# Block-sparse attention and its expert layers on one core: scores from 64-row tiles of TensorE, and the first product cut in two around the values

## The chip, the core and the metric

One core of a Trainium2 chip runs the whole kernel as one program. The metric is the device time of one execution in microseconds (us). TensorE's granted clock is written as a share of full speed; its two levels are 1.2 and 2.4 GHz. Five engines run programs of their own, in order: PE (TensorE), DVE (VectorE), ACT (ScalarE), POOL (GpSimd) and SP (SyncE, which here only issues DMAs).

## The reference, cut to what matters

```python
B, H, S, D = 4, 8, 768, 64             # float32; block = 32, so 24 blocks
scores = q @ k^T / sqrt(D)             # kept where mask, else -1e9
# mask: blocks at most 1 apart; the first and the last block, as rows and as columns;
# and for each query block 3 sampled key blocks
attn = softmax(scores); o = attn @ v
x = o as [B*S, H*D] = [3072, 512]
h = x @ w_in                           # 512 x 2048
g = h * erf(softplus(h))
out = g @ w_out                        # 2048 x 512
```

## The kernel before, in words

**Attention, in units.** A batch has 16 units (`units`, line 775). Ten are of kind "m": one of five tiles of 128 queries (four blocks of 32, number `j`) by one of two quads of heads. A quad is two pairs of heads (`r`), a pair is two heads (`a`), and the two heads of a pair lie on partitions 0 to 63 and 64 to 127 of the transposed queries and keys. For its own block of queries each head needs 256 key columns: 96 of the three neighbouring blocks, 96 of the three sampled blocks (copied side by side into `kg` by POOL, `gather`), and 64 of the first and the last block (`key_columns`, line 554). Four units "f" (one pair each; the first and the last block, which see all 768 keys) and two units "e" (the two remaining blocks beside the end) finish the batch.

**Scores (`scores`, line 565).** The two heads of a pair are done by one product over all 128 partitions. For this the queries of a block stand block-diagonally in `qm` (line 131): 64 columns, of which 32 belong to head 0 and are zero on the partitions of head 1, and the other way round. `qm` is zeroed once; `order_q` (line 146) copies each loaded tile `qt` into its diagonal blocks with two copies of 64 partitions. An m unit is 24 products (2 pairs x 3 column parts x 4 blocks), each 128 x 64 stationary, and blocks with even and odd `j` write the two halves of the output's partitions. All operands are float32, and a float32 product is issued as two weight loads and two matmul instructions, both of the same tile, one directly behind the other. The scores of a unit take two PSUM banks of a single buffer (`ps_s`, line 94), so the next unit's scores wait until the exponentials of this one are read out.

**Behind the scores.** `soft_max` (DVE: maximum, bias), `soft_exp` (ACT: four exponentials, one rounding copy), `soft_low` (DVE: rest of the rounding), `soft_turn` (SP: transpose by DMA). Two units later `values` (line 605) multiplies with the gathered values `vb` (96 small products of 128 x 32 stationary, float16) into `po`, a single PSUM buffer, `norm` (DVE) divides, and `turn` makes the rows of the expert layers.

**Expert layers, in groups.** There are 96 groups (4 batches x 3 chunks of 256 rows x 8 parts of 256 hidden columns). `ff_first` (line 686) makes `h` (two sets `j` of 12 products with 256 columns), `ff_logs` is five ACT instructions, `ff_power` one of DVE, `ff_exp` one of ACT, `ff_gate` three of DVE, and `ff_second` (line 735), two groups later, 12 products of 512 columns.

**The order of the work** is written by hand, and every engine keeps it (`InOrder`, line 49). After the first four units and the decoding of the weights (lines 875 to 973) the loop at line 978 runs one step per group, and most steps also have a unit. On PE such a step is: first product, values, scores, second product. On DVE it is: gate of the step before, norm, maximum and bias, `order_q` of the next tile in every second unit (`next_queries`, line 804), power, rest of the output, `soft_low`. On SP it is: writes, gathers of values, query load, transposes. `until` (line 977) sets in which steps a unit starts.

Of the kernel before, what the change touches and what calls it, by code (L numbers as in the profile page):

```python
# [42 lines left out]
def sparse_attention_moe(ctx: ExitStack, tc: tile.TileContext, qT, kT, v, sampled, w_in, w_out, out):  # L43
# [86 lines left out]
    qts = {}  # L130
    qm = cp.tile([P, HP, 4, 2, BLOCK], F32, tag="qm", name="qm")
    pool.memset(qm, 0.0)

    def load_q(b, t):
        place, tag, bufs = (mo, "g", FF_LAG + 1) if b == 0 and t in (1, 2) else (ld, "qt", 1)
        qt = place.tile([P, HP, P], F32, tag=tag, name=f"qt_{b}_{t}", bufs=bufs)
        rows = qT[b].rearrange("(r t) d s -> (t d) r s", t=2)
        if t < MT:
            c = (1 + 4 * t) * BLOCK
            sp.dma_start(qt, rows[:, :, c : c + P])  # L140
        else:
# [423 lines left out]
    def scores(unit):  # L565
        kind, b, n = unit[0], unit[1], unit[2:]
        tag = "_".join(str(x) for x in unit)
        s = ps_s.tile([P, 1024], F32, tag="s", name=f"s_{tag}")
        if kind == "m":

            t, quad = n
            s4 = s.rearrange("p (h r w) -> p h r w", h=2, r=2)
            for r in range(2):
                pr = 2 * quad + r
                for part in range(3):
                    for j in range(4):
                        o = slice((j % 2) * 64, (j % 2) * 64 + 64)
                        q_ = qm[:, pr, j].rearrange("p a c -> p (a c)")
                        c, e, keys = key_columns(b, 1 + 4 * t + j, slice(0, P), pr)[part]
                        pe.matmul(s4[o, j // 2, r, c:e], q_, keys, start=True, stop=True)  # L580
            softs[unit] = (s, 4, 256)
        elif kind == "e":
            (quad,) = n
            s3 = s.rearrange("p (r w) -> p r w", r=HP)
            for r in range(2):
                for part in range(3):
                    for j in range(2):
                        o = slice(j * 64, j * 64 + 64)
                        q_ = qm[:, 2 * quad + r, j].rearrange("p a c -> p (a c)")
                        c, e, keys = key_columns(b, NB - 3 + j, slice(0, P), 2 * quad + r)[part]  # L590
                        pe.matmul(s3[o, r, c:e], q_, keys, start=True, stop=True)
# [13 lines left out]
    def values(b, t, quad):  # L605
        po = ps_po.tile([P, 4, D + 1], F32, tag="po", name=f"po_{b}_{t}_{quad}")
        for hl in range(4):
# [5 lines left out]
            for x, ln in ((0, 0), (0, 1), (1, 0)):  # L613
                for half in range(2):
                    for j in range(4):
                        if t < MT:
                            pT = pts["m", b, t, quad][:, ((j // 2) * 2 + r) * 4 + x * 2 + half]
                            col = (j % 2) * 64 + a * 32
                            vg = vb[:, slot_of[b, 1 + 4 * t + j]]
                        elif j in (1, 2):  # L620
                            pT, col = pts["e", b, quad][:, r * 4 + x * 2 + half], (j - 1) * 64 + a * 32
                            vg = vb[:, slot_of[b, NB - 4 + j]]
                        else:
                            continue
                        w = slice(c, c + D + 1) if ln == 0 else slice(c + D + 2, c + VW)
                        todo[j].append((pT[:, col : col + 32], vg[:, half, w]))
                if t == MT:
                    for k in range(KT):
                        for j in (0, 3):
                            pT, col = pts["f", b, pr][:, x * KT + k], (0 if j else 64) + a * 32  # L630
                            w = slice(c, c + D + 1) if ln == 0 else slice(c + D + 2, c + VW)
                            todo[j].append((pT[:, col : col + 32], vb[:, slot_of[b, -1 - k // 2], k % 2, w]))
# [52 lines left out]

    def ff_first(b, ch, fg):
        tag = f"{b}_{ch}_{fg}"
        isg = first_scale(b)
        h = ps_h.tile([P, W], F32, tag="h", name=f"h_{tag}")
        xT = xTs[b, ch].rearrange("p n u c -> p n (u c)")  # L690
        for j in range(FG):
            f = fg * FG + j
            hj = h[:, j * CW : (j + 1) * CW]
            for kt in range(NK):
# [5 lines left out]
                pe.matmul(hj, lo, xa, start=False, stop=kt == NK - 1)  # L700
        ffs[b, ch, fg] = (h, isg)

    ffs = {}
# [100 lines left out]
    def next_queries(m):  # L804

        b, n = divmod(m, per)
        if n < 10 and n % 2 == 1:
            order_q(b, n // 2 + 1)
            if n < 9:
                load_q(b, n // 2 + 2)  # L810
        if n == per - 1 and b + 1 < B:
            order_q(b + 1, 0)
            load_q(b + 1, 1)

    def behind(m):

        b, n = divmod(m, per)
        if b + 1 < B:
            c = b + 1
            if n == 10:  # L820
                load_q(c, 0)
            k = n if b else 2 * (n - 10) if n > 9 else -1
# [60 lines left out]
    load_q(0, 1)  # L883
    load_q(0, 2)
    for n in range(3):
# [7 lines left out]
    place_v(0, 1, 1)  # L893
    order_q(0, 0)
    have_k.add(0)
# [21 lines left out]
    scores(units[1])  # L917
    used_keys(units[1])
    gathers(0)
    for i in range(10, 16):  # L920
# [4 lines left out]
    soft_exp(units[1])  # L925
    order_q(0, 1)
    work("Qi1 Di2 Qi2 Di3 Qi3")
# [11 lines left out]
    scores(units[3])  # L939
    used_keys(units[3])  # L940
    work("Qi6 Di7 Qi7 Do0")
    set_apart()
# [13 lines left out]
    turn(*seen(units[1]))  # L956
    order_q(0, 2)
    soft_low(units[3])
# [10 lines left out]
    gathers(0)  # L969
    load_q(0, 3)  # L970
    begun = FIRST
# [6 lines left out]
    for m in range(len(groups) + FF_LAG):  # L978
# [35 lines left out]
        if unit:  # L1014
            soft_max(unit)
            next_queries(begun - 1)
        if group:
# [56 lines left out]
```

## Time and profile before

| | us |
|---|---|
| median of 3 runs (lowest, highest) | 838.58 (835.89, 844.72) |
| the profiled execution | 838.56 |
| its span in the profile | 836.8 |
| PE busy in it | 710.8 |
| ACT busy | 601.1 |
| DVE busy | 554.4 |

The profiled execution lies at the median of the runs, and 1.8 us of it lie outside the span. The first 90 us set up (loads, decoding of the weights, the first four units), the rest is the loop over the groups. The first two dozen steps of the loop still carry work on the weights.

### The profile page before, as it was taken

To read this page: it belongs to the slowest core of one execution; us is meant where nothing else is said; L and a number is where in the kernel's file an instruction comes from. 1 tells how busy PE (TensorE), PEld (TensorE's weight loads), DVE (VectorE), ACT (ScalarE), POOL (GpSimd) and SP (SyncE) were. 2 spreads that over 40 slices of the span, in tenths; PEclk is the share of its full clock that TensorE was granted. 3 is DMA by queue.
4 is the path that set the end of the run, shared out by engine and by line. 5 is a ranking of instruction groups with operands and counts; after the bars stand their busy time and mean duration, and the time that the engine had idled before them with its cause. 6 is when DMAs were issued, how large, how long until landed. Compare 5 with 4: busy or idle time off the path is not lost.

```text
span 836.8 us, 26712 instructions
## 1 busy us (share of the span) xinstructions
PE 710.8 (85%) x11100; PEld 504.8 (60%) x11100; DVE 554.4 (66%) x977; ACT 601.1 (72%) x999; POOL 123.7 (15%) x344
## 2 busy tenths in 40 slices
PE   1253637899897899899999899999999899999997
PEld 1252424566665667566777666667777576766664
DVE  3994796887764766766566676756677567654454
ACT  4654657987865766887768778868678678776774
POOL 5430111001222220100201231000111100000000
PEclk9775867989998999999999999999999999999999
DMA  8999953687899697661497886633576758211000
GB/s 325 297 257 318 243 120 90 164 207 164 172 212 209 178 205 198 186 131 45 136 216 178 210 198 192 167 79 83 117 167 166 190 103 188 53 33 40 1 27 26
DMA packets 199930, 131.61 MB, mean 157 GB/s; under 512 B 144000, under 2 KB 167168, under 8 KB 199808
## 3 DMA queue, kind: packets, MB, share of 16 engines
q1 hardware_dynamic: 196384, 118.10, 58.1%
q0 software_dynamic: 3424, 11.80, 4.3%
q8 instruction: 87, 1.43, 0.7%
q14 instruction: 35, 0.29, 0.1%
HBM read 83.88 MB, written 12.95 MB: 116 GB/s over the span
## 4 chain that ended last, share of the span: by engine, by line
PE 47%; DVE 15%; issue 12%; ACT 10%; DMA 10%; SPq 2%; POOL 2%; POOLq 1%; ACTq 0%
PE h L59 18%; PE o L59 18%; PE s_m L59 5%; DMA vb<-vtab 4%; PE po L59 3%; DVE g L59 2%; ACT pf_m L59 2%; DVE q L59 2%; DVE mx_m L59 2%; DMA vtab<-vn 2%; SPq L59 2%; ACT x L59 2%; DVE p_m L59 2%; POOL kg L59 2%; ACT q L59 2%
## 5 line engine op out<-in xcount | busy, mean ns | idle before, releaser
L59 PE MATMUL h<-xT,wi 128*128 128x256 f16 x2304 | 274.2, 276 | 14.9 <-ACT wi L59 7.5
L59 PE MATMUL o<-wo,g 128*128 128x512 f16 x1152 | 270.3, 385 | 7.9 <-DVE wo L59 4.0
L59 PEld LDWEIGHTS <-wi 128*128 128x128 f16 x2304 | 227.4, 99 | 65.5 <-ACT wi L59 8.8
L59 PEld LDWEIGHTS <-g 128*128 128x128 f16 x1152 | 110.3, 99 | 133.0 <-issue 14.8
L59 ACT ACTIVATE x<-x 128x512 f32<-128x512 f32 x288 | 181.5, 630 | 9.1
L59 POOL COPY kg<-kx 128x128 f32 x264 | 90.5, 394 | 286.2 <-PE s_m L59 183.6
L59 ACT ACTIVATE pf_m<-s_m,nb_m 128x256 f32<-128x256 f32 x160 | 62.7, 475 | 65.4 <-DVE nb_m L59 59.5
L59 DVE SCALAR_TENSOR_TENSOR q<-x,q 128x512 f32<-128x512 f32 x96 | 66.7, 695 | 61.4 <-ACT x L59 60.1
L59 ACT ACTIVATE x<-h,isg 128x512 f32<-128x512 f32 x96 | 65.2, 680 | 36.3 <-PE h L59 35.7
L59 PE MATMUL s_m<-kx,qm 128*64 128x64 f32 (+1 forms) x1280 | 75.0, 249 | 6.8 <-ACT pf_m L59 4.2
L59 ACT ACTIVATE q<-q 128x512 f32<-128x512 f32 x96 | 59.5, 620 | 29.6 <-DVE q L59 29.6
L59 DVE SCALAR_TENSOR_TENSOR q<-q,h 128x512 f32<-128x512 f32 x96 | 65.5, 682 | 22.6 <-ACT q L59 22.6
L59 DVE TENSOR_TENSOR p_m<-pf_m,p_m 128x1024 f16<-128x1024 f32 x40 | 49.3, 1232 | 32.3 <-ACT p_m L59 32.3
L59 DVE SCALAR_TENSOR_TENSOR g<-q,g 128x512 f16<-128x512 f32 x96 | 67.0, 698 | 3.3
L59 PE MATMUL po<-vb,pT_m 128*32 128x65 f16 (+1 forms) x3840 | 44.7, 201 | 25.7 <-DMA vb<-vtab 15.0
L59 PEld LDWEIGHTS s_m<-kx,qm 128*64 128x64 f32 x1280 | 59.7, 146 | 10.4 <-ACT pf_m L59 4.9
L59 ACT ACTIVATE q<-x 128x512 f32<-128x512 f32 x96 | 60.5, 630 | 3.1
L59 DVE TENSOR_REDUCE mx_m<-s_m 128x4 f32<-128x1024 f32 x40 | 48.8, 1219 | 20.2 <-PE s_m L59 20.2
L59 PEld LDWEIGHTS <-pT_m 128*32 128x32 f16 x3840 | 38.0, 97 | 36.8 <-DMA vb<-vtab 16.3
L59 PE MATMUL s_m<-kg,qm 128*64 128x96 f32 x640 | 46.9, 261 | 3.2 <-POOL kg L59 2.2
L59 DVE TENSOR_TENSOR x<-xf,x 128x512 f16<-128x512 f32 x24 | 16.9, 703 | 43.3 <-ACT x L59 43.3
L59 DVE TENSOR_SCALAR g<-q 128x512 f16<-128x512 f32 x96 | 41.3, 431 | 3.3
(115 smaller groups left out, 623.7 us busy)
## 6 DMA issues: line engine op xcount, KB each, us to landing
vb<-vtab SPq DMA_DIRECT2D x280, 65.0 KB, 2.9
vb<-vtab SPq DMA_DIRECT2D x32, 390.0 KB, 4.1
vraw<-in_v_dram SPq DMA_DIRECT2D x10, 768.0 KB, 5.1
vtab<-vn SPq DMA_DIRECT2D x16, 390.0 KB, 5.4
vb<-vtab SPq DMA_DIRECT2D x12, 520.0 KB, 5.0
qt<-in_qT_dram SPq DMA_DIRECT2D x20, 256.0 KB, 3.3
out_dram<-wo SPq DMA_DIRECT2D x20, 256.0 KB, 4.3
vb<-vtab SPq DMA_DIRECT2D x36, 130.0 KB, 3.0
```

Source lines behind the costliest of these rows:

```text
L59: done = call(*args, **kwargs)
```

## The change

The diagonal tile `qm` and `order_q` go. Scores are made from the loaded queries `qt` directly, which now has two buffers. In an m unit, four products per unit (one for each pair and head) take the 64 partitions of one head and all 128 queries against the first and the last key block; then 32 products take 64 partitions and the 32 queries of one block, for the neighbour and the sampled part, with the four blocks on the four quarters of the output's partitions and the two heads in the two PSUM banks. Units "e" and "f" are made of the same small tiles, with both heads in one bank. `values` reads the transposed scores at the new places. A query tile is loaded after the scores of the unit in which its buffer comes free, and `next_queries` now stands directly behind `scores`. `ff_first` takes the list of sets to make: in a step set 0 is made, then the values, then set 1 and the logarithms, then the scores.

```diff
-    qm = cp.tile([P, HP, 4, 2, BLOCK], F32, tag="qm", name="qm")
-    pool.memset(qm, 0.0)
...
-        place, tag, bufs = (mo, "g", FF_LAG + 1) if b == 0 and t in (1, 2) else (ld, "qt", 1)
-        qt = place.tile([P, HP, P], F32, tag=tag, name=f"qt_{b}_{t}", bufs=bufs)
+        qt = ld.tile([P, HP, P], F32, tag="qt", name=f"qt_{b}_{t}", bufs=2)
...
-    def order_q(b, t):
-        qt = qts.pop((b, t)).rearrange("p r (j c) -> p r j c", c=BLOCK)
-        copy = act.copy if b == 0 and t in (1, 2) else dve.tensor_copy
-        for a in range(2):
-            copy(qm[a * D : (a + 1) * D, :, :, a, :], qt[a * D : (a + 1) * D])
...
             t, quad = n
-            s4 = s.rearrange("p (h r w) -> p h r w", h=2, r=2)
+            qt = qts[b, t]
+            s4 = s.rearrange("p (a r w) -> p a r w", a=2, r=2)
+            for pr, r, a in ((2 * quad + n // 2, n // 2, n % 2) for n in range(4)):
+                rows = slice(a * D, (a + 1) * D)
+                pe.matmul(s4[:, a, r, 192:], qt[rows, pr], kxs[b][rows, 0 : NB : NB - 1, pr, :], start=True, stop=True)
+            for r in range(2):
+                pr = 2 * quad + r
+                for part in range(2):
+                    for j in range(4):
+                        o = slice(j * BLOCK, (j + 1) * BLOCK)
+                        for a in range(2):
+                            rows = slice(a * D, (a + 1) * D)
+                            c, e, keys = key_columns(b, 1 + 4 * t + j, rows, pr)[part]
+                            pe.matmul(s4[o, a, r, c:e], qt[rows, pr, o], keys, start=True, stop=True)
+            softs[unit] = (s, 4, 256)
...
-            q_ = qm[:, pr, 2:].rearrange("p n a c -> p (n a c)")
             for c, e in ((0, 512), (512, S)):
-                keys = kxs[b][:, c // BLOCK : e // BLOCK, pr, :]
-                pe.matmul(s[:, c:e], q_, keys, start=True, stop=True)
+                for a in range(2):
+                    rows = slice(a * D, (a + 1) * D)
+                    keys = kxs[b][rows, c // BLOCK : e // BLOCK, pr, :]
+                    pe.matmul(s[a * 64 : a * 64 + 64, c:e], qts[b, MT][rows, pr, 64:], keys, start=True, stop=True)
...
-        if n < 10 and n % 2 == 1:
-            order_q(b, n // 2 + 1)
-            if n < 9:
-                load_q(b, n // 2 + 2)
-        if n == per - 1 and b + 1 < B:
-            order_q(b + 1, 0)
-            load_q(b + 1, 1)
+        if n in (1, 3, 5, 7):
+            load_q(b, n // 2 + 2)
+        elif n in (9, 15) and b + 1 < B:
+            load_q(b + 1, n // 15)
...
         if group:
-            ff_first(*group)
-            ff_logs(*group)
+            ff_first(*group, (0,))
         if place:
             values_of(place)
+        if group:
+            ff_first(*group, (1,))
+            ff_logs(*group)
         if steps:
             gathers(begun)
         if unit:
             scores(unit)
             used_keys(unit)
+            next_queries(begun - 1)
...
         if unit:
             soft_max(unit)
-            next_queries(begun - 1)
```

## Rows read from the trace of the kernel before

**Rows 1.** The page: busy time by engine; PE and its clock in 40 slices.
```profile
PE 710.8 (85%) x11100; PEld 504.8 (60%) x11100; DVE 554.4 (66%) x977; ACT 601.1 (72%) x999; POOL 123.7 (15%) x344
...
PE   1253637899897899899999899999999899999997
...
PEclk9775867989998999999999999999999999999999
```

**Rows 2.** Timeline of PE, a step with a unit and one without (start, length).
```profile
414.13 2.78 PE L59 MATMUL h<-xT,wi 128*128 128x256 f16 x24
416.84 0.96 PE L59 MATMUL po<-vb,pT_m 128*32 128x65 f16 x96
417.73 0.55 PE L59 MATMUL s_m<-kx,qm 128*64 128x96 f32 x8
...
419.67 2.76 PE L59 MATMUL o<-wo,g 128*128 128x512 f16 x12
422.27 2.78 PE L59 MATMUL h<-xT,wi 128*128 128x256 f16 x24
424.89 2.75 PE L59 MATMUL o<-wo,g 128*128 128x512 f16 x12
```

**Rows 3.** The same timeline in slices of 0.02 to 0.05 us.
```profile
417.73 0.30 PE L59 MATMUL s_m<-kx,qm 128*64 128x96 f32 x2
...
417.73 0.39 PE L59 MATMUL s_m<-kx,qm 128*64 128x96 f32 x4
...
417.73 0.47 PE L59 MATMUL s_m<-kx,qm 128*64 128x96 f32 x6
...
365.31 0.59 PE L59 MATMUL s_f<-kx,qm 128*128 128x512 f32 x1
...
365.31 1.02 PE L59 MATMUL s_f<-kx,qm 128*128 128x512 f32 x2
```

**Rows 4.** Groups by shape: busy us, mean ns | idle before, releasers.
```profile
L59 PE MATMUL s_m<-kg,qm 128*64 128x96 f32 x640 | 46.9, 261 | 3.2 <-POOL kg L59 2.2 <-POOL vn L59 1.0
...
L59 PEld LDWEIGHTS s_m<-kx,qm 128*64 128x64 f32 x1280 | 59.7, 146 | 10.4 <-ACT pf_m L59 4.9 <-issue 4.1
...
L59 PEld LDWEIGHTS s_f<-kx,qm 128*128 128x128 f32 x64 | 11.0, 192 | 11.9 <-issue 7.6 <-ACT pf_m L59 2.2 <-ACT pf_e L59 1.8
...
L59 DVE COPY qm<-qt 64x512 f32<-64x512 f32 x44 | 20.7, 470 | 0.5 <-DMA qt<-in_qT_dram 0.2
```

**Rows 5.** Timeline of DVE in the step of rows 2.
```profile
418.63 0.68 DVE L59 SCALAR_TENSOR_TENSOR q<-q,h 128x512 f32<-128x512 f32 x1
...
425.37 1.23 DVE L59 TENSOR_TENSOR p_m<-pf_m,p_m 128x1024 f16<-128x1024 f32 x1 [2.19 <-ACT p_m L59]
426.51 0.68 DVE L59 SCALAR_TENSOR_TENSOR q<-q,h 128x512 f32<-128x512 f32 x1
```

**Rows 6.** Who waited for whom: us in total, times, longest.
```profile
DVE mx_m L59 <- PE s_m L59: 20.2, 16, 5.0
...
PE po L59 <- DMA vb<-vtab: 15.0, 7, 8.0
...
PE po L59 <- DMA pT_m<-p_m: 7.8, 6, 3.5
```

**Rows 7.** The chain that ended last, single pieces: start, length, what.
```profile
110.21 0.41 DVE qm L59
...
393.69 1.94 PE s_m L59 x48
...
653.08 3.92 DMA pT_m<-p_m
...
686.19 1.98 PE s_m L59 x48
...
713.86 1.29 PE s_f L59 x4
```

More of the change, by code (lines that the diff above doesn't have):

```diff
@@ L571, in scores @@
             t, quad = n
-            s4 = s.rearrange("p (h r w) -> p h r w", h=2, r=2)
+            qt = qts[b, t]
[13 more added lines that the diff above has]
+            softs[unit] = (s, 4, 256)
+        elif kind == "e":
+            (quad,) = n
+            qt = qts[b, MT]
+            s3 = s.rearrange("p (r w) -> p r w", r=HP)
             for r in range(2):
@@ L575, in scores @@
                 for part in range(3):
[L576 to L586, printed above, removed]
-                    for j in range(2):
[L588 to L591, printed above, removed]
+                    for j in range(2):
+                        for a in range(2):
+                            rows, o = slice(a * D, (a + 1) * D), j * 64 + a * BLOCK
+                            c, e, keys = key_columns(b, NB - 3 + j, rows, pr)[part]
+                            q_ = qt[rows, pr, j * BLOCK : (j + 1) * BLOCK]
+                            pe.matmul(s3[o : o + BLOCK, r, c:e], q_, keys, start=True, stop=True)
             softs[unit] = (s[:, :512], 2, 256)
@@ L594, in scores @@
             (pr,) = n
-            q_ = qm[:, pr, 2:].rearrange("p n a c -> p (n a c)")
             for c, e in ((0, 512), (512, S)):
-                keys = kxs[b][:, c // BLOCK : e // BLOCK, pr, :]
-                pe.matmul(s[:, c:e], q_, keys, start=True, stop=True)
+                for a in range(2):
+                    rows = slice(a * D, (a + 1) * D)
+                    keys = kxs[b][rows, c // BLOCK : e // BLOCK, pr, :]
+                    pe.matmul(s[a * 64 : a * 64 + 64, c:e], qts[b, MT][rows, pr, 64:], keys, start=True, stop=True)
             softs[unit] = (s[:, :S], 1, S)
@@ L616, in values @@
                         if t < MT:
-                            pT = pts["m", b, t, quad][:, ((j // 2) * 2 + r) * 4 + x * 2 + half]
-                            col = (j % 2) * 64 + a * 32
+                            pT = pts["m", b, t, quad][:, (a * 2 + r) * 4 + x * 2 + half]
+                            col = j * BLOCK
                             vg = vb[:, slot_of[b, 1 + 4 * t + j]]
@@ L629, in values @@
                         for j in (0, 3):
-                            pT, col = pts["f", b, pr][:, x * KT + k], (0 if j else 64) + a * 32
+                            pT, col = pts["f", b, pr][:, x * KT + k], a * 64 + (32 if j == 0 else 0)
                             w = slice(c, c + D + 1) if ln == 0 else slice(c + D + 2, c + VW)
@@ L684, in first_scale, with ff_first @@
         return ff_scales[b]
-    def ff_first(b, ch, fg):
+    def ff_first(b, ch, fg, parts):
         tag = f"{b}_{ch}_{fg}"
         isg = first_scale(b)
-        h = ps_h.tile([P, W], F32, tag="h", name=f"h_{tag}")
+        if 0 in parts:
+            ffs[b, ch, fg] = (ps_h.tile([P, W], F32, tag="h", name=f"h_{tag}"), isg)
+        h = ffs[b, ch, fg][0]
         xT = xTs[b, ch].rearrange("p n u c -> p n (u c)")
-        for j in range(FG):
+        for j in parts:
             f = fg * FG + j
@@ L700, in ff_first @@
                 pe.matmul(hj, lo, xa, start=False, stop=kt == NK - 1)
-        ffs[b, ch, fg] = (h, isg)
     ffs = {}
@@ L819, in behind @@
             c = b + 1
-            if n == 10:
-                load_q(c, 0)
             k = n if b else 2 * (n - 10) if n > 9 else -1
@@ L883, in sparse_attention_moe @@
     load_q(0, 1)
-    load_q(0, 2)
     for n in range(3):
@@ L893, in sparse_attention_moe @@
     place_v(0, 1, 1)
-    order_q(0, 0)
     have_k.add(0)
@@ L918, in sparse_attention_moe @@
     used_keys(units[1])
+    next_queries(1)
     gathers(0)
@@ L925, in sparse_attention_moe @@
     soft_exp(units[1])
-    order_q(0, 1)
     work("Qi1 Di2 Qi2 Di3 Qi3")
@@ L940, in sparse_attention_moe @@
     used_keys(units[3])
+    next_queries(3)
     work("Qi6 Di7 Qi7 Do0")
@@ L956, in sparse_attention_moe @@
     turn(*seen(units[1]))
-    order_q(0, 2)
     soft_low(units[3])
@@ L969, in sparse_attention_moe @@
     gathers(0)
-    load_q(0, 3)
     begun = FIRST
```

## The prediction

> **What bounds the kernel now.** I read the page first [rows 1]: PE is busy for 710.8 of 836.8 us, ACT and DVE are at 72% and 66%, and from the tenth slice on PE shows nine tenths in most slices at full clock. The idle time of PE thus lies in the set-up; in the loop it is the first candidate. The timeline of PE then gives the price list of a step [rows 2]. With a unit: first product 2.71 us (414.13 to 416.84), values 0.89, scores 1.94, second product 2.60, together 8.14. Without: 2.62 and 2.60, together 5.22. The reader is to see that the first product takes 0.09 more when values follow than when the second product does: a change of tile shape on PE costs about 0.09 us.
>
> The second candidate is the round over DVE and ACT. In the same step the gate begins at 418.63 and that of the next step at 426.51 [rows 5]: 7.88 us through gate, norm, maximum, exponentials, rounding copy and rest (425.37). It waits for PE nowhere in this round, so two steps with units in a row cannot come closer than about 7.9 us whatever PE does. A step without a unit lets DVE catch up.
>
> The chain of waits tells which of the two sets the end [rows 7]. From 393.69 to 686.19 it runs over the scores of 15 m units on PE (first and last shown), and over three more before (at 91.60, 218.41 and 291.17): 18 of the 36 m units that start in the loop. In the others it runs over DVE, ACT, POOL or a DMA.
>
> **The change part by part. Scores of an m unit.** The slices of the timeline show how float32 products on half tiles run [rows 3]: the first two end 0.30 us after the start, four 0.39, six 0.47 and eight 0.55 ([rows 2]), so two instructions of 96 columns run side by side and two more follow every 0.083 us (0.25 / 3). In an f unit, on one whole tile, the second instruction of a product ends 0.43 us after the first (0.59, 1.02): the two instructions of one product cannot overlap. The two that start together above are therefore of two different tiles, though the program has the second half of the same product between them. So each tile works off its own instructions. With eight tiles (two halves of partitions, four quarters of the output) the 32 products of 96 columns are 64 instructions, eight per tile: 8 x 0.083 = 0.66 us, against 16 products on two tiles, 1.33 us, before. Below 0.66 it cannot fall, as each tile streams its columns; above stand 1.33 (only four tiles at once) and 2.65 (one product per 0.083).
>
> The four products with the first and last block have all 128 queries as weights. Loads of 64 float32 columns show 146 ns, of 128 columns 192 ns [rows 4]: 0.72 ns per column, 0.09 us for 128 columns, which I round to 0.1. Their eight instructions stream 64 columns (0.055 us, two thirds of 0.083), so the load is the longer part. On two tiles side by side that is 4 x 0.1 = 0.40 us; it lies between 0.22 (loads hidden) and 0.80 (one after the other). Before, the same columns were sixteen instructions, some 0.45 us. The scores so take 0.40 + 0.09 (new change of tile shape inside the unit) + 0.66 + 0.05 (first load) + 0.09 = 1.29 us instead of 1.94: 0.65 less (bounds 0.88 less and 0.42 more).
>
> **The first product in two halves.** Two sets of 1.31 us instead of 2.62, and one change of shape more: +0.09 per step with values. Net an m step loses 0.56 us on PE. The e and f steps with values (8) pay 0.09 = 0.7 us; their scores I leave as they are, since their diagonal tiles stream as many columns per tile as the whole tiles did (f: 1.29 us, [rows 7]).
>
> **What of it counts.** On the chain: 18 x 0.56 = 10.1 us. In the 18 others the round over DVE and ACT stays; but DVE waits 20.2 us in all for scores [rows 6], and values also come 1.4 us earlier in their step, so I count half: 5.0 us (bounds 0 and 10.1).
>
> **Copies of queries.** 44 copies of 470 ns on DVE go [rows 4], 0.94 per pair. They lie between the bias and the power, and while ACT makes exponentials and the rounding copy DVE waits anyway (2.19 us in [rows 5]); if that cover is gone they cost their 0.94. While the weights are still decoded DVE has no such gap, and two pairs lie on the chain (the first at 110.21, [rows 7]): 2 x 0.85 = 1.7 us. The copies of ACT, the zeroing on POOL and one early query load lie beside waits for other loads: nothing.
>
> **Query loads and SP.** The load now waits for the scores instead of the copies. Behind it on SP stand the transposes of the same unit, which wait for the rest of the output, later in any case. Nothing, within one DMA issue. Two loads move further: that of tile 2 of the first batch from the first burst to behind the second unit's scores, that of tile 3 forward past SP's loads of weights; both tiles are needed only units later.
>
> **Values before half of the first product.** This is the cost. Thirteen times values wait for a DMA (7 for gathered values, 6 for transposes, 22.8 us, [rows 6]). Before, all of the first product ran ahead of that wait; now 12 products, 1.31 + 0.09 = 1.40 us, stand behind it, and the five logarithms on ACT behind them. Three of these waits lie on the chain in the second half of the run, one at 653.08 [rows 7]: 3 x 1.40 = +4.2 us (bounds 0 and 13 x 1.40 = 18.2).
>
> **The sum**, against the profiled execution of 838.6 us, which is also the median: -10.1 - 5.0 - 1.7 + 4.2 + 0.7 = -11.9, so 827 us. Its own range is 809 (all 36 steps at 0.79 less, 0.88 without the split's 0.09, the copies, no late values: 838.6 - 28.4 - 1.7) to 835.
>
> **The rivals. The round over DVE and ACT takes the gain.** If the steps off the chain give nothing, and half of what those on it give returns as waits for the exponentials, 838.6 - 5.0 - 1.7 + 4.2 + 0.7 = 837 us. For it: 7.88 us per round against the 8.14 of PE [rows 2, 5], so 0.26 us is all that a second unit step in a row can win. Against: steps without a unit lie between from the third chunk on.
>
> **Late values (the other side).** With PE ahead, more of the 44 steps with values meet a DMA that has not landed, and each holds back 1.40 us. At 20 on the chain it is 28.0 us against a gain of 16.1 (10.1 + 5.0 + 1.7 - 0.7): 850 us. The sign turns at 12. For it: 13 wait already; against: most of those lie where a new batch's values are still being written, not in the regular steps, whose values take 0.89 with no wait.
>
> **Both heads in one bank.** In f and e units the two halves of the partitions write one bank. If such tiles take turns, an f unit costs a second 1.29 us; ten of the sixteen lie on the chain (one at 713.86, [rows 7]), and as the unit grows more will: thirteen give 16.8 us. An e unit costs a second 0.88 (8 x 0.083 + 4 x 0.055), six give 5.3: 827 + 22.1 = 849 us. No row shows two row tiles at all. The Trainium skill (TensorEngine Tiling (Array Packing), Gotcha 1: PSUM Pressure) says that different row tiles cannot use the same bank at the same time; by that rule this rival holds. I give it little because the two halves here write different partitions.
>
> **Half rows take turns everywhere.** Then blocks 1.33, ends 0.80: scores 2.36 us, +0.51 with the split per m step, x 36 = 18.4; f units +1.29 x 16 = 20.6; minus the copies 1.7: 876 us.
>
> **Products strictly in order.** If a matmul may not start before the one ahead of it has, each product on these tiles costs 0.083: 2.65 + 0.5 + 0.23 = 3.4 us, +1.5 with the split per m step, 54 us, and f +0.43 x 16 = 7, less the copies 1.7: 898 us. Against it speak the pairs that start together [rows 3], where strict order would start one alone. The Trainium skill (TensorE: Matmul & The Clock Gate, Part 3: Packing small matmuls, "What overlaps and what doesn't") states that order; by it this rival's 898 us would come. The trace disagrees: two instructions run from the first 0.02 us on and the next two follow 0.09 later.
>
> **How the numbers follow.** Forecast 0.54, the round takes it 0.19, late values 0.08, one bank 0.09, half rows in turn 0.05, strict order 0.05. A measurement of this kernel tells some 1% (8.4 us) from no change. Of the forecast 0.47 lies below 830.2 and 0.07 within 1%; with the first rival same is 0.26; the other four are slower by over 1%, 0.27. The range reaches from 809 to 850, over the forecast's own (809 to 835) and the two nearer slow rivals, and leaves out the last two and the far half of those.
>
> **What would show it.** Right: the gathered-part products on 64 x 32 tiles, eight starting within 0.1 us, some 0.66 us per unit, scores near 1.3 us, an m step near 7.6 us on PE where nothing waits; the copies gone from DVE; waits of PE for DMAs at values about as many as now. Wrong: two or four starts at a time; f units of 2.5 us; more than some twelve late values; DVE and ACT rounds of 7.9 us with PE waiting for exponentials in each. The granted clock stays at its upper level (2.4 GHz) in the loop as now [rows 1]; if it fell in more slices than now, the sum is too low.

## The result, and the profile after

The changed kernel takes 848.66 us (median of 4 runs, 847.01 to 849.25), the kernel before on the same chip 838.18: a ratio of 1.0104 (95% interval 1.0056 to 1.0153). The forecast was 827 us, so the direction was wrong; the time lies just inside the range, near its upper end.

The page of the changed kernel (busy time by engine, PE and its clock in 40 slices, the instruction queue of the DMAs, the chain by engine):

```profile
PE 708.1 (84%) x12316; PEld 475.1 (56%) x12316; DVE 536.2 (63%) x933; ACT 597.4 (71%) x995; POOL 120.9 (14%) x343
...
PE   1253547799897889899999799899999799999997
...
PEclk9999757989998999999999999999999899999999
...
q8 instruction: 96, 1.57, 0.8%
...
PE 41%; DVE 18%; ACT 17%; DMA 13%; issue 6%; SPq 4%; POOL 0%; ACTq 0%; POOLq 0%
```

Beside [rows 1], the copies are gone from DVE (18 us less), yet PE is busy only 2.7 us less, and PE has 1,216 matmuls and as many weight loads more. Of the chain PE holds 41% (47 before) and ACT 17% (10): part of the path has moved from PE to ACT (the page before: `PE 47%; DVE 15%; issue 12%; ACT 10%`).

The timeline of PE in an m step in which nothing waits:

```profile
431.82 1.47 PE L59 MATMUL h<-xT,wi 128*128 128x256 f16 x12
433.23 1.05 PE L59 MATMUL po<-vb,pT_m 128*32 128x65 f16 x96
434.21 1.49 PE L59 MATMUL h<-xT,wi 128*128 128x256 f16 x12
435.63 0.99 PE L59 MATMUL s_m<-kx,qt 64*128 64x64 f32 x24
436.41 0.37 PE L59 MATMUL s_m<-kg,qt 64*32 64x96 f32 x16
...
437.15 2.77 PE L59 MATMUL o<-wo,g 128*128 128x512 f16 x12
439.75 2.78 PE L59 MATMUL h<-xT,wi 128*128 128x256 f16 x24
```

From start to start: 1.41, 0.98, 1.42, then scores 1.52 (435.63 to 437.15), second product 2.60. Together 7.93 us where [rows 2] had 8.14. The scores did shrink (1.94 to 1.52), but the cut first product with its values takes 3.81 instead of 3.60. What is left per m step is 0.21 us, not the 0.56 forecast.

Two narrow windows, at the first blocks of that unit and at the start of an f unit:

```profile
436.41 0.29 PE L59 MATMUL s_m<-kg,qt 64*32 64x96 f32 x8
...
363.74 0.65 PE L59 MATMUL s_f<-kx,qt 64*64 64x512 f32 x2
```

Eight matmuls of eight tiles start within 0.05 us, and the two heads of an f unit start together though they write one bank.

The waits (who waited for whom: total, times, longest), beside [rows 6]:

```profile
ACT x L59 <- PE h L59: 83.7, 51, 9.0
...
DVE mx_m L59 <- PE s_m L59: 20.8, 11, 4.3
PE po L59 <- DMA pT_m<-p_m: 19.8, 9, 5.2
PE po L59 <- DMA vb<-vtab: 18.0, 10, 7.1
```

Values waited 22.8 us for DMAs before and 37.8 now, and ACT's logarithms, behind the second half of the product, waited 35.7 us for it before and 83.7 now. DVE waits for scores as long as it did. Waits of an engine are not yet time on the chain; the runs below put a price on each part of the change. What they showed first is a wait that no line of the prediction had.

### The profile page after: what moved, and what is told of

Read it like the earlier page. It is cut to its first block, busy times and chain, and to the rows that moved or that the text cites. A ratio compares the mean times of both kernels' runs of the same rounds, so it can differ in the third digit from the quotient of the medians.

```text
span 845.3 us, 29083 instructions
## 1 busy us (share of the span) xinstructions
PE 708.1 (84%) x12316; PEld 475.1 (56%) x12316; DVE 536.2 (63%) x933; ACT 597.4 (71%) x995; POOL 120.9 (14%) x343
## 4 chain that ended last, share of the span: by engine, by line
PE 41%; DVE 18%; ACT 17%; DMA 13%; issue 6%; SPq 4%; POOL 0%; ACTq 0%; POOLq 0%
PE h L59 17%; PE o L59 16%; ACT x L59 5%; DMA vb<-vtab 4%; SPq L59 4%; PE po L59 3%; DVE g L59 3%; DVE q L59 3%; DMA vraw<-in_v_dram 3%; ACT q L59 3%; ACT pf_m L59 3%; DVE mx_m L59 3%; DMA vtab<-vn 3%; DVE p_m L59 2%; DMA pT_m<-p_m 2%
## 5 line engine op out<-in xcount | busy, mean ns | idle before, releaser
L59 PE MATMUL h<-xT,wi 128*128 128x256 f16 x2304 | 287.3, 279 | 15.7 <-ACT wi L59 7.0
L59 PE MATMUL o<-wo,g 128*128 128x512 f16 x1152 | 268.2, 382 | 5.4 <-ACT wo L59 3.0
L59 PEld LDWEIGHTS <-wi 128*128 128x128 f16 x2304 | 225.5, 100 | 70.4 <-ACT wi L59 8.4
L59 ACT ACTIVATE x<-x 128x512 f32<-128x512 f32 x288 | 181.4, 630 | 9.1
L59 PEld LDWEIGHTS <-g 128*128 128x128 f16 x1152 | 108.3, 98 | 135.3 <-issue 14.7
L59 POOL COPY kg<-kx 128x128 f32 x264 | 85.0, 372 | 290.1 <-PE s_m L59 184.4
L59 ACT ACTIVATE x<-h,isg 128x512 f32<-128x512 f32 x96 | 65.2, 680 | 83.8 <-PE h L59 83.7
L59 DVE SCALAR_TENSOR_TENSOR q<-x,q 128x512 f32<-128x512 f32 x96 | 67.0, 698 | 70.6 <-ACT x L59 70.3
L59 ACT ACTIVATE pf_m<-s_m,nb_m 128x256 f32<-128x256 f32 x160 | 62.5, 472 | 30.9 <-DVE nb_m L59 26.8
L59 PE MATMUL po<-vb,pT_m 128*32 128x65 f16 (+1 forms) x3840 | 46.6, 206 | 42.6 <-DMA pT_m<-p_m 19.8
L59 ACT ACTIVATE q<-q 128x512 f32<-128x512 f32 x96 | 59.5, 620 | 29.5 <-DVE q L59 29.5
L59 DVE SCALAR_TENSOR_TENSOR q<-q,h 128x512 f32<-128x512 f32 x96 | 65.5, 682 | 22.6 <-ACT q L59 22.6
L59 PEld LDWEIGHTS <-pT_m 128*32 128x32 f16 x3840 | 39.6, 101 | 54.2 <-DMA pT_m<-p_m 22.5
L59 DVE TENSOR_TENSOR p_m<-pf_m,p_m 128x1024 f16<-128x1024 f32 x40 | 49.7, 1243 | 31.1 <-ACT p_m L59 29.2
L59 DVE SCALAR_TENSOR_TENSOR g<-q,g 128x512 f16<-128x512 f32 x96 | 67.0, 698 | 3.3
L59 PE MATMUL s_m<-kx,qt 64*32 64x96 f32 (+1 forms) x1600 | 62.7, 274 | 6.7 <-ACT pf_m L59 4.6
L59 ACT ACTIVATE q<-x 128x512 f32<-128x512 f32 x96 | 60.5, 630 | 3.0
L59 DVE TENSOR_REDUCE mx_m<-s_m 128x4 f32<-128x1024 f32 x40 | 48.7, 1217 | 20.9 <-PE s_m L59 20.8
L59 PEld LDWEIGHTS s_m<-kx,qt 64*32 64x32 f32 (+1 forms) x1600 | 45.0, 129 | 19.6 <-issue 10.3
L59 DVE TENSOR_TENSOR x<-xf,x 128x512 f16<-128x512 f32 x24 | 16.7, 696 | 55.6 <-ACT x L59 55.6
L59 DVE TENSOR_SCALAR g<-q 128x512 f16<-128x512 f32 x96 | 41.2, 429 | 3.3
L59 ACT ACTIVATE p_m<-pf_m 128x1024 f16<-128x1024 f32 x40 | 42.3, 1057 | 1.3
```

What stands on the lines that cost most here:

```text
L59: done = call(*args, **kwargs)
```

## The experiments

Each run is read by four numbers of its profile: the number of TensorE instructions recorded; the start of the loop's first group; the *program waits* (defined with the second experiment); and the rest of the loop, that is the span less the other two. Each profile is one execution, whose rest can differ by some 3 us from the next one's (before: 741.5 and 738.2, mean 739.9). Where it lay more than 3 us off its kernel's median this is said. Kernels are compared by the ratio: the kernel before took 838.18 us beside the changed one and 842.8 to 843.4 beside the others.

| kernel | median us | ratio to before | instr. | start | program waits | rest |
|---|---|---|---|---|---|---|
| before, two profiles | 838 to 843 | 1 | 22,299 | 87.2, 88.6 | 8.1, 11.9 | 741.5, 738.2 |
| changed | 848.66 | 1.0104 (1.0056 to 1.0153) | 24,737 | 90.7 | 8.4 | 746.2 |
| split_only | 844.93 | 1.0034 (1.0002 to 1.0065) | 22,299 | 90.6 | 3.9 | 750.3 |
| values_first | 852.90 | 1.0129 (1.0094 to 1.0164) | 22,299 | 89.9 | 3.9 | 756.5 |
| small_whole | 853.34 | 1.0152 (1.0119 to 1.0185) | 24,737 | 92.6 | 20.6 | 738.1 |
| small_f | 847.62 | 1.0054 (1.0036 to 1.0072) | 24,609 | 92.5 | 20.9 | 733.1 |
| f_diag | 850.54 | 1.0103 (1.0071 to 1.0135) | 24,609 | 92.1 | 11.8 | 742.6 |
| phase | 856.78 | 1.0189 (1.0118 to 1.0260) | 24,864 | 90.6 | 20.1 | 746.0 |
| ends32 | 882.96 | 1.0464 (1.0413 to 1.0514) | 26,657 | 95.0 | 67.1 | 728.8 |
| scores_first | 853.03 | 1.0128 (1.0084 to 1.0171) | 24,732 | 91.0 | 20.1 | 740.8 |
| spread | 850.27 | 1.0079 (1.0043 to 1.0116) | 24,719 | 91.2 | 9.7 | 747.0 |
| vlast_small | 848.77 | 1.0076 (1.0047 to 1.0104) | 24,608 | 91.1 | 20.8 | 735.8 |
| vlast_before | 851.12 | 1.0101 (1.0061 to 1.0141) | 22,303 | 90.7 | 13.0 | 751.7 |
| vlast_shift | 840.24 | 0.9969 (0.9935 to 1.0003) | 24,783 | 93.6 | 7.0 | 743.8 |
| one_later | 858.46 | 1.0181 (1.0139 to 1.0223) | 24,739 | 92.3 | 3.3 | 761.5 |

**1. One part at a time: the scores (small_whole), the order (split_only).** The first is the changed kernel with this edit, the second the kernel before with its reverse:

```diff
-            ff_first(*group, (0,))
-        if place:
-            values_of(place)
-        if group:
-            ff_first(*group, (1,))
+            ff_first(*group, (0, 1))
             ff_logs(*group)
+        if place:
+            values_of(place)
```

> The changed kernel with the old order of a step (whole first product and logarithms, then values, then scores); scores from 64-row tiles stay. Theory (the order is what costs: the cut is 0.21 us per step with values, 44 steps, and late values gained 15.0 us of waiting): 0.2 x 44 = 9 us and some 8 of late values go, so 830 to 836 us, ratio to before 0.990 to 0.998, an m step without waits 0.2 us shorter on PE. Rival (scores from small tiles, the set-up or the e and f units cost): 843 us or more.

> The kernel before with the new order alone: half of the first product, values, the other half; scores still from block-diagonal queries over all 128 rows. Theory (the order costs): 0.2 x 44 = 9 us, of which half or more on the chain, and more and dearer waits of values for DMAs: 845 to 855 us, ratio to before 1.008 to 1.020. Rival (the scores, set-up or e and f units cost): 836 to 842 us, ratio 0.998 to 1.004.

Measured: 853.34 and 844.93 us. The theory failed for the first: with the old order the small tiles are not faster by 1% but slower by 1.5%, by the medians worse than with the new one (1.0152 and 1.0104, whose intervals overlap). Each part alone costs, and the two together seem to cost less than the scores alone. That suggested that one part relieves something that the other causes.

**2. More small tiles (ends32): what the tiles cost.** The four products with 128 columns of queries become sixteen of 32 columns. The expectation says that the new order is kept, but the kernel as built also goes back to the old order, so small_whole, and not the changed kernel, is the one to compare it with:

```diff
-            for pr, r, a in ((2 * quad + n // 2, n // 2, n % 2) for n in range(4)):
...
-                for part in range(2):
+                for part in range(3):
...
-            ff_first(*group, (0,))
+            ff_first(*group, (0, 1))
+            ff_logs(*group)
         if place:
             values_of(place)
-        if group:
-            ff_first(*group, (1,))
-            ff_logs(*group)
```

> The changed kernel, new order kept, with the first and last block's columns of an m unit made in sixteen products on the eight 64x32 tiles, as a third part of the loop, in place of four products with 128 columns of queries. Theory (each tile streams its own instructions, and a change of tile shape costs 0.09): four more instructions of 64 columns per tile, 4 x 0.055 = 0.22 us for 0.59, scores 1.52 to about 1.15 us, -0.37 x 36 steps, half of it counted: 839 to 844 us. Rival (the issue of small products limits, about 0.013 us per matmul instruction as in the second half of a unit now; 96 instead of 72 instructions): scores 1.4 to 1.6 us, 847 to 851 us.

Measured: 882.96 us, far outside both, and 3.1% more than small_whole by the ratios (the profiled execution, 892.76 us, lies 10 us above the median). The timeline of PE in one of its units, and its waits:

```profile
527.84 0.96 PE L59 MATMUL po<-vb,pT_m 128*32 128x65 f16 x96
528.73 0.40 PE L59 MATMUL s_m<-kx,qt 64*32 64x96 f32 x16
...
529.50 0.34 PE L59 MATMUL s_m<-kg,qt 64*32 64x96 f32 x7
533.81 0.38 PE L59 MATMUL s_m<-kg,qt 64*32 64x96 f32 x3 [3.96 <-issue]
```

```profile
PE s_m L59 <- issue: 56.4, 24, 4.2
```

In the middle of a unit, between two products of one kind, PE stands for 3.96 us and the profile names no releaser ("issue"). Twenty-four such waits make 56.4 us. I numbered the recorded TensorE instructions in order of time: the instruction behind such a wait has a number that is 193 modulo 256, again and again (16,321 here, then 16,833; 19,393, 19,905, 20,417 later). The page's line of the instruction queue says why 256: it moved 87 packets in the kernel before, 96 in the changed one, 104 here, 16 KB each, and 22,299, 24,737 and 26,657 instructions divided by 256 are 87.1, 96.6 and 104.1. Each packet is a piece of 256 instructions of TensorE's program. In all of these waits (31 of over 0.55 us here, 8 before, 10 in the changed kernel) PE starts again 1.2 to 1.7 us after the end of one packet (the packets taken in order, the first of them for position 449), and at no such position in the loop of any of the sixteen profiles does PE go on less than 1.2 us after its packet's end. PE waits for its own program. From here on *program waits* are the gaps of over 0.48 us from one TensorE start to the next that end at such a number, less 0.1 us each, from 88 us on.

In the 158 longer waits of all profiles PE starts a piece 3.7 us (median; 3.1 to 4.9 for the middle eight tenths) after it started the piece before. That is no threshold: 103 other pieces began within 3.7 us of the one before and had no such wait. A step of the old order with small tiles has values and scores side by side, 192 and 144 instructions in 2.5 us: more than one piece. Block-diagonal scores were 96 instructions. In ends32 they are 192 and 192. The new order puts 24 instructions of 1.4 us between values and scores, and the program waits are 20.6 us with the old order and 8.4 with the new. How much of this difference is the order and how much the place where the pieces begin is not separated: the next run has the new order and 20.1 us, and no run moved the old order.

The Trainium skill (Runtime: NRT & Kernel Launch, section "Instruction fetch mechanics") says that an engine's program comes in 16 KiB blocks of 256 instructions, the next fetched while the current one runs, and that the cost of crossing a block is "mostly hidden". The block size agrees with the packets here; the second half does not hold where the code is this dense: 56.4 us are not hidden.

**3. Does the wait belong to the product or to its number (phase)?** Thirty-two tiny products in the set-up, 128 instructions, whose result nobody reads:

```diff
+    idle = ps_h.tile([P, 512], F32, tag="h", name="idle")
+    for i in range(32):
+        pe.matmul(idle[:1, :1], one, one, start=True, stop=True)
```

> The changed kernel with 32 tiny products added during the set-up (one value each, 128 instructions on TensorE in all, while it waits for loads); nothing else. In the traces so far the unexplained waits of TensorE in the loop all stand ahead of an instruction whose number in TensorE's own stream is 193 modulo 256 (9409 and 15041 before; 6593, 10689 and 16065 after; 449 modulo 512 in 21 of the 24 long ones of the kernel with 32-column ends). Theory (TensorE waits for its own program, which arrives in pieces of 256 instructions): the waits stay at 193 modulo 256 of the stream and so move to other products, 128 earlier in the code; the time stays within 6 us of the changed kernel (843 to 855), either way. Rival (these waits belong to the products, as by a busy bank or a semaphore): the same products wait, their number now 65 modulo 256.

Measured: 856.78 us, 8.1 more than the changed kernel (0.85% by the two ratios, 7 us), outside the band named; the intervals of the two ratios overlap, so the times alone do not prove the step. The long waits stayed at 193 modulo 256 (14 over 0.55 us in the loop) and fell on other products, such as these two in the values of the last tile of the second and third batches, where the changed kernel has none (pieces of the chain):

```profile
412.87 2.99 issue
...
600.99 2.20 issue
```

Program waits rose from 8.4 to 20.1 and the rest of the loop stayed (746.2, 746.0). In the loop nothing but the place of the piece boundaries changed. So of the two placings the changed kernel as it stood had the better one.

**4. The same from the other side (vlast_small, vlast_before, vlast_shift).** An order that cuts nothing and keeps 2.6 us of long products on both sides of values and scores:

```diff
         if m >= FF_LAG:
             for u in range(CT):
                 ff_second(*groups[m - FF_LAG], u)
+        if place:
+            values_of(place)
+        if steps:
+            gathers(begun)
```

This stands in vlast_small, on the changed kernel with f units on block-diagonal queries, and in vlast_before, on the kernel before; norm and turn move to the next step.

> Scores from 64-row tiles in m and e units, f units on block-diagonal queries, and in a step the whole first product, scores, whole second product, then values (norm and turn in the step behind). 2.6 us of long products now stand on both sides of values and of scores and nothing is cut. Theory (TensorE waits for its program where 256 instructions run in less than some 3.4 us, and late values cost the rest): waits at 193 modulo 256 under 6 us for 20.6 with values and scores side by side, waits of values for DMAs under 15 us; loop without these waits 738.1 - 3.6 (f units) + 4 (one more change of tile shape in 44 steps) - some 8 (late values) = 730; with set-up 91: 823 to 833 us, ratio to before 0.98 to 0.99. Rival (the round over DVE and ACT bounds the loop): 840 us or more, PE waiting for exponentials.

> The kernel before with that order alone (first product, scores, second product, values), scores from block-diagonal queries. Theory: waits at 193 modulo 256 under 4 us for 8.1, late values under 15 us for 22.8, one more change of shape: 741.5 + 4 - 6 + 4 = 743 in the loop, 91 before it: 833 to 840 us, and some 8 to 12 us over the same order with small tiles, which is what the small tiles save once code and values don't wait. Rival (small tiles save nothing): equal to that kernel within 4 us.

Both missed: 848.77 and 851.12 us. Late values fell (PE waited 11.6 us for gathered values in vlast_before and not at all for transposes), but vlast_small still had 20.8 us of program waits, 8 of 12 now in the steps of e and f units or in the values of the last tile, which are 192 products, 384 instructions. The profile of vlast_before lies 6 us above its median, so its rest isn't to be leaned on. Then vlast_small with the idle products of phase, 44 of them (`range(44)`), 176 instructions:

> The order product, scores, product, values with small tiles (median 848.8, of whose loop 20.8 us are waits at 193 modulo 256) with 44 tiny products added in the set-up, 176 instructions, nothing else. Replaying that kernel's own trace with pieces of 256 instructions that come 3.0 to 3.4 us after the piece before was begun gives 9 to 12 us of such waits as it stands and 2 to 3 us with the stream moved by 176. Theory (where the pieces begin decides): such waits 4 to 10 us, so 835 to 842 us, ratio to before 0.988 to 0.998. Rival (such waits come from the load on the DMA engines, wherever the pieces begin): 15 us or more of them, 845 to 852 us.

Measured: 840.24 us, 8.5 less than without them (1.07% by the ratios, 9 us), and 7.0 us of program waits. The theory held, and here the intervals of the two ratios are apart; the fastest kernel of the study is thus level with the one before (the interval of its ratio includes 1). Its profile lies 6 us above its median, and its rest is 8.0 us longer than that of vlast_small, so the two profiles alone show less of the gain than the times do.

**5. The f units (f_diag), and the scores alone (small_f).** A half-size `qm` for f units; then the old order with it:

```diff
+            q_ = qm[:, pr].rearrange("p n a c -> p (n a c)")
-                for a in range(2):
-                    rows = slice(a * D, (a + 1) * D)
-                    keys = kxs[b][rows, c // BLOCK : e // BLOCK, pr, :]
...
+                keys = kxs[b][:, c // BLOCK : e // BLOCK, pr, :]
+                pe.matmul(s[:, c:e], q_, keys, start=True, stop=True)
```

> The changed kernel with the f units alone back on block-diagonal queries and whole 128-row tiles (64 x 512 copies of four tiles, two copies each of half the size, stay for them). Theory (an f unit of small tiles costs 0.25 us more: 1.44 for 1.29 and 0.09 in the first product ahead of it): 16 x 0.25 = 4 us less, copies at most +2: 843 to 847 us. Rival (the f units cost nothing on the chain): 847 to 850 us.

> The changed kernel with the old order and with f units on block-diagonal queries: only the scores of m and e units and the query loads differ from before. If the terms add up: loop without waits for the program 738.1 - 3.6 = 734.5 (before 741.5 and 738.2 in two profiles), with some 20 us of such waits for 8 to 12 before: 846 to 850 us, ratio to before 1.004 to 1.010; the gain of the small tiles on TensorE is thus 4 to 7 us and is given back by the waits for its program. Rival (the waits for the program hide other waits and so cost less than their sum): 836 to 843 us.

f_diag: the rest of the loop fell by 3.6 us as expected (about as much as two profiles of one kernel differ), but the ratio did not (1.0103 for 1.0104): program waits rose from 8.4 to 11.8. Each f unit has eight instructions fewer, so the pieces begin elsewhere. small_f: 847.62 us, rest 733.1, program waits 20.9, all three as the sum had it. This is the cleanest reading of the small tiles: without the f units they give 739.9 - 733.1 = 6.8 us on the loop, and the program takes back 10.9 (20.9 less the mean 10.0 of the kernel before).

**6. What the order costs (values_first).** The kernel before with values ahead of the whole product, nothing cut:

```diff
+        if place:
+            values_of(place)
         if group:
             ff_first(*group)
             ff_logs(*group)
-        if place:
-            values_of(place)
```

> The kernel before (block-diagonal scores) with the values ahead of the whole first product: nothing is cut, but the logarithms begin one run of values (0.9 us) later and late values hold back all of the product. Theory D (the new order costs by the delay of the logarithms and by late values, less by the cut): at least as slow as half product, values, half product, whose loop without waits for the program is 750.3: 748 to 758 here, 844 to 854 us. Theory C (the cut itself, 0.21 us in 44 steps, is the cost): the loop without those waits is 738 to 745 as before, 838 to 844 us.

Measured: 852.90 us, rest 756.5; theory D. Its waits:

```profile
ACT x L59 <- PE h L59: 94.1, 56, 8.6
...
DVE mx_m L59 <- PE s_m L59: 34.5, 16, 6.2
...
PE po L59 <- DMA pT_m<-p_m: 28.9, 8, 9.4
...
PE po L59 <- DMA vb<-vtab: 18.9, 11, 8.4
```

ACT waits for the product, DVE for the scores, and values for DMAs, each longer than before. So an order can cost this much with nothing cut; the 0.9 us by which the logarithms start later in each such step and the late values are not told apart here. That the cut itself costs nothing is not shown: it is 0.21 us in each step with values on PE.

**7. Other orders, none faster.** scores_first (product, scores, values), spread (product, scores, half of the second product, values, other half), one_later (the changed order around the values of the unit before). The cores of the three edits:

```diff
         if unit:
             scores(unit)
...
+        if place:
+            values_of(place)
```

```diff
+        if m >= FF_LAG:
+            ff_second(*groups[m - FF_LAG], 0)
+        if place:
+            values_of(place)
...
-            for u in range(CT):
-                ff_second(*groups[m - FF_LAG], u)
+            ff_second(*groups[m - FF_LAG], 1)
```

```diff
+        place, pend = pend, place
```

> The changed kernel with the order whole first product, scores, values, second product; on DVE the maximum ahead of the norm. Theory A (late values are what the change pays: 37.8 us of waiting for DMAs ahead of values against 22.8): values stand 1.5 us later, few wait, less than 15 us of such waits, and 835 to 843 us. Theory B (TensorE waits for its own program where values and scores stand side by side, 336 instructions in 2.5 us): waits at 193 modulo 256 stay at some 20 us as in the kernel with the old order, and 848 to 855 us.

> The changed kernel with the order whole first product, scores, half of the second product, values, other half of the second product; on DVE the maximum ahead of the norm. Theory A and B together: values stand 2.9 us later so that few wait for a DMA, and 1.3 us of long products stand between scores and values, so that the program arrives in time (under 10 us of waits at 193 modulo 256): 828 to 838 us, faster than both kernels. If neither counts and the round over DVE and ACT bounds: 843 to 850 us.

> The changed kernel with the values (norm and turn with them) one step later; the first product stays cut in two around them, now around the values of the unit before. Theory (of what the new order costs, 0.2 x 44 = 9 us is the cut itself, and what transposes that are not there yet hold back comes on top): the waits of values for transposes (19.8 us) fall under 5, those for gathered values stay near 18, the loop without waits for the program falls from 746.2 by 3 to 8 us: 840 to 846 us. Rival (the cut is all that the order costs): loop without those waits 745 to 748, 846 to 850 us.

scores_first: 853.03 us, with 20.1 us of program waits and 28.5 us of waits of values for DMAs: B for the time, and A's count of late values was wrong. spread: 850.27 us; program waits were under 10 as expected (9.7), but the rest is 747.0. one_later: 858.46 us, outside both: no wait for transposes is left, but waits for gathered values doubled, from 18.0 to 36.9 us. I read that as the slots of `vb` coming free a step later too; no run tested it. PE also waited 12.0 us for the gathered keys `kg` there (2.1 in the changed kernel).

**8. The set-up (before_again).**

> The kernel before, unchanged, for a second profile of it. In its first profile the loop's first group begins at 87.2 us; in eight other kernels' profiles at 90.6 to 95.0, that with the new order alone (set-up untouched) at 90.6. Theory (the set-up varies from one execution to the next, and the first profile was a short one): 89 to 93 us now, the loop behind it 748 to 752 us. Rival (the changed kernels' set-up is 3 us longer): 87 to 88 us.

The first group began at 88.6 us, between theory and rival. Kernels with the old set-up begin at 87.2, 88.6, 89.9, 90.6 and 90.7 us, those with the changed one at 90.6 to 92.6 (leaving out ends32 at 95.0 and vlast_shift at 93.6). Whether 1 or 2 us of the loss come from the set-up is not settled.

## Why the prediction was wrong, point by point

By the profiles the loss of 7.5 us (845.3 less 837.8, the mean span of two profiles of before) is: small tiles in m and e units, with nearly all copies gone, -6.8 (small_f less before); f units +5.0 (small_whole less small_f); order +8.1 (changed less small_whole); program waits -1.6 (8.4 less 10.0); start of the loop +2.8 (90.7 less 87.9), part of it chance. Each term is a difference of single profiles and good to some 3 us.

**What a shorter unit is worth: the step that turned the sign.** "18 x 0.56 = 10.1 us" and "so I count half" booked each unit's saving in 27 of the 36 steps. For the scores alone that is 27 x 0.65 = 17.6 us, and 19.2 with the copies; 6.8 came, and 7.7 in the pair that has the new order (f_diag less split_only). The 12.4 us that are missing are more than the whole loss of 7.5: with them the kernel would have been faster. Half of them is size, 27 x (0.65 - 0.42) = 6.2 us. The other half is the count: 18 x 0.42 = 7.6 would use up the 6.8, so nothing is left for the 18 other steps. The half there was counted because DVE waits 20.2 us for scores; that wait is 19.1 us in small_f (`DVE mx_m L59 <- PE s_m L59: 19.1, 15, 5.1`) and 20.8 in the changed kernel. Nor did the chain stay where it was: before, it runs over the scores of 18 m units of the loop (17 in the second profile), in small_f of 14, in the changed kernel of 9. With shorter scores other work takes its place on the chain, as the rival of the round over DVE and ACT had it for the steps off the chain; which work does so is not isolated by any run.

**Scores of an m unit: mechanism right, size off.** All eight tiles run side by side, so the two rivals of half rows in turn and of strict order fall. 1.29 us were forecast, 1.52 came. The ends took 0.59 with the change of shape inside the unit, against 0.49: their matmuls start 0.111 us apart, where 0.1 was put. The blocks took 0.84, against 0.66: the 32 matmuls of the first sixteen products start eight at a time, later ones singly.

**The cut: 0.09 was put, 0.21 came.** The first product takes 2.83 instead of 2.71, the values 0.98 instead of 0.89.

**E and f units: "their scores I leave as they are" was wrong, the second step that failed.** f_diag and small_f put the sixteen f units at 3.6 to 5.0 us, 0.2 to 0.3 each: 1.44 us for 1.29, and one more change of shape. The rival of the shared bank falls nevertheless: it wanted a second 1.29 us. The Trainium skill (TensorEngine Tiling (Array Packing), Gotcha 1: PSUM Pressure) would have had them take turns; the two starts shown above disagree.

**The new order: dearer than put, by 1 to 3 us.** With the cut in every step with values the forecast has 4.2 + 27 x 0.09 + 0.7 = 7.3 us for it. Three pairs of kernels that differ in the order alone put it at 8.1, 9.5 (f_diag less small_f) and 10.4 us (split_only less before), cut included; how much of that is cut and how much late values is not separated. Some eleven steps of the loop have late values where the kernel before has seven (the thirteen waits of [rows 6] include those of the set-up), not the twenty of the rival that came closest in time (850): that its 850 us lie near 848.66 is chance. But one can be dearer than 1.40. PE around one of them, in the changed kernel, then before:

```profile
655.35 1.47 PE L59 MATMUL h<-xT,wi 128*128 128x256 f16 x12
662.00 1.50 PE L59 MATMUL po<-vb,pT_m 128*32 128x65 f16 x96 [5.18 <-DMA pT_m<-p_m]
663.44 2.74 PE L59 MATMUL h<-xT,wi 128*128 128x256 f16 x12
666.11 1.01 PE L59 MATMUL s_m<-kx,qt 64*128 64x64 f32 x8
...
667.98 2.33 PE L59 MATMUL o<-wo,g 128*128 128x512 f16 x10
```

```profile
650.71 2.78 PE L59 MATMUL h<-xT,wi 128*128 128x256 f16 x24
657.04 1.47 PE L59 MATMUL po<-vb,pT_m 128*32 128x65 f16 x96 [3.54 <-DMA pT_m<-p_m]
658.44 0.91 PE L59 MATMUL s_m<-kx,qm 128*64 128x96 f32 x8
...
661.37 2.76 PE L59 MATMUL o<-wo,g 128*128 128x512 f16 x12
```

Scores start 1.40 us after the values before, 4.11 after them now: 2.71 held back, not 1.40. Stretches (PE busy, granted clock, DMA) say why; the first two are of the changed kernel, the third of the kernel before:

```profile
652.70:655.30 2.60, 2.60 (x22) 1.00 0.68 209
662.00:666.10 4.10, 4.10 (x108) 0.50 0.80 195
...
657.00:660.40 3.40, 3.36 (x124) 0.52 0.98 242
```

Behind the wait the granted clock is 0.50, its lower level (1.2 GHz), and the held-back half of the product runs there: 2.67 us where 1.42 is its time at 2.4 GHz. In the kernel before, the whole product ran ahead of the wait at full clock, and the scores at the lower one (0.52), 2.93 us for 1.94. So by the start of the second product the difference is only 1.65 us (4.33 us after the values began before, 5.98 now): the shorter scores give part of it back. Not every wait does this: values at 345.92 of the kernel before came after one of 1.43 us, took their 0.96 us, and the granted clock behind them (347.0 to 349.5) was 1.00.

**Copies and query loads.** Their price was not measured alone; the copies are inside the 6.8 us. No run tested the moved loads.

**What the prediction did not have at all.** It priced products by their time on the array and never counted their instructions. Products added on small tiles are four instructions each, and the program's arrival was a bound of its own: with the old order it takes back 10.9 us, more than the 6.8 that the small tiles give. In the changed kernel's profile it costs nothing net (8.4 us for 10.0); with the pieces elsewhere it was 20.1 (phase). Whether the cut order or the placing made the 8.4 is open.

## What to carry to other kernels

A saving per unit is worth its size only where the unit stays on the chain: here 6.8 us arrived where the 0.42 us measured in a unit, in the 27 steps counted, and the copies would have made 13.0. Count the instructions per microsecond that a change makes: where 256 of them were due in less than some 3 to 5 us TensorE could wait for its program (though 103 pieces begun within 3.7 us had no such wait), and more, smaller tiles made such stretches. Compare two versions at more than one placing of the code before a 1% difference is believed: 176 idle instructions alone made one kernel here some 9 us faster, and 128 made another some 7 us slower by its median. Work placed behind a possible wait is to be priced at the clock that TensorE has after the wait.

## What the hardware did that was not expected

- TensorE waited for its program: up to 67.1 us in one kernel's profile, always at the same position in pieces of 256 instructions, 3.96 us in the row shown. Why the position is 193 and not 0 no run tells.
- Eight float32 products on eight 64x32 tiles run side by side past the second halves that stand between them in the program: eight starts within 0.05 us. The Trainium skill (TensorE: Matmul & The Clock Gate, Part 3: Packing small matmuls, "What overlaps and what doesn't") states a strict order, by which the scores would have taken some 3.4 us; they took 1.52.
- Two row tiles that write different partitions of one PSUM bank started together (f units, 1.44 us in all).
